# GpSimd shifts tied to vector instructions that read PSUM, with a late shift open to the vector engine, in a fused attention and MLP kernel

## The chip, the cores and the metric

The kernel runs on one NeuronCore of a Trainium2 chip. Five instruction streams run side by side and meet through semaphores: TensorE (PE, with its weight loads shown as PEld), VectorE (DVE), ScalarE (ACT), GpSimd (POOL) and SyncE (SP, which issues the DMAs). The metric is the device time of one execution in microseconds. Three runs of the kernel before gave 782.16, 782.68 and 783.34 us; their median, 782.68 us, is the time before.

## The reference

The input x has 2048 rows of 512 values. It is normalised (no learned scale), and the result xn feeds two branches that are added to x:

```
xn = layernorm(x)
q = xn @ wq            # 32 heads of 16
k = xn @ wk            # one head of 16, shared by all query heads
v = xn @ wv
p = softmax(q k^T / 4)
o = (p v) @ wo
h = gelu(xn @ w1 + b1) # 1792 wide
y = h @ w2 + b2
out = x + o + y
```

The attention is the larger part: 32 heads x 2048 queries x 2048 keys of scores, each of which needs an exponential.

## The kernel before

**Tiles.** Scores are computed transposed, 128 keys by 512 queries of one head at a time: one *tile*, one PSUM bank. There are 4 blocks of 512 queries, 8 groups of 4 heads and 16 key blocks for each, hence 2048 tiles. Three tiles make a *unit*; there are 683 units. `scores(u)` issues a unit's three matmuls (line 934) into banks 0 to 2 or 3 to 5, alternately, so a unit's banks must be emptied before the unit after next can be computed. Bank 6 collects the product with V for one group of four heads, bank 7 serves everything else (query projections, MLP).

**Two ways to the exponential.** A character of the string `DTAB` says for each unit which of its tiles take which way. Most tiles go through ScalarE's exponential (line 957, tile `E`). The others, called D tiles, go through VectorE and cost ScalarE nothing. VectorE first evicts the scores from PSUM to 16-bit integers (line 988, called p1 in the planner), which read as bf16 are a coarse exponential. Copies of this integer tile with added constants (+26, +51, +77, -26), each multiplied by V with a weight of its own and summed in PSUM, sharpen it. So a D tile feeds five matmuls (line 1001, `Dt`) against one for an `E` tile.

**The copies and the shift.** Line 1034 makes the copies on VectorE, for a *batch* of 1 to 6 D tiles at once: one instruction copies buffer 0 to buffer 1 with +26, the next copies buffers 0 and 1 to buffers 2 and 3 with +51. Then buffer 0 itself is shifted in place by -26 (line 1031), one instruction of 128x512 per tile, on GpSimd. The shift has to wait for both copies and for the matmul that reads the unshifted buffer; the fifth matmul waits for the shift. `CLOSE` letters of `DTAB` and the limit `KB` set where a batch ends.

**The planner.** `Prog.add` records each operation with its engine, dependencies, a cost (`occ`), a latency (`lat`) and an allowance; `Prog.schedule` then runs a list schedule at build time and fixes the order of instructions on each engine, and `emit` writes the streams with the semaphore waits. At run time every stream is in order: a TensorE matmul that waits for a shift holds up every matmul behind it, the next scores included. Evictions of scores have the most negative allowance on VectorE (`P1_ALLOW`), so they go first among what is ready. TensorE takes scores (kind `S`) when they are ready and otherwise products with V or side work; it gets filler matmuls (line 1305) where the planner sees a gap.

**The shifts in the planner.** Operations marked `lock` are VectorE instructions that read and write SBUF (the copies, the square of the queries, the normalisation of an output). The planner keeps them from starting before `lockend`, which is set from the end of a running shift. A shift (kind `pl`) is placed in one of two ways. When VectorE takes an operation without `lock` of at least `PL_WIN` (0.4 us in the plan), one ready shift is started beside it, and waits for the last `lock` operation or the one before it through a semaphore, the *gate*. A shift that has been ready for `PL_MAX` (2 us in the plan) is taken by GpSimd without a gate:

```
return max(o.rdy, lockend) if o.lock else o.rdy + PL_MAX if o.kind == "pl" else o.rdy
```

**The side work.** Query projections for the next block, the MLP's first product, the GELU (done by ScalarE in two stretches, after units 182 and 512, since its table must be swapped) and the MLP's second product are placed by unit numbers in `QK`, `HP`, `GU` and `YP`.

Of the kernel before, what the change touches and what calls it, by code (L numbers as in the profile page):

```python
# [33 lines left out]
S_WAIT = 0.1  # L34
P_WAIT = 0.0
PL_OCC = 0.62
PL_LAT = 0.07
PL_GATE = 0.0
PL_WIN = 0.4
PL_MAX = 2.0  # L40
PL_START = -0.07
PL_SEM = 0.16
PL_FREE = 0.135
# [12 lines left out]
DMASK = {".": (), "0": (0,), "2": (2,), "a": (0, 1), "b": (1, 2), "x": (0, 1, 2),  # L56
         "o": (0,), "t": (2,), "A": (0, 1), "B": (1, 2), "X": (0, 1, 2)}
CLOSE = "otABX"
DTAB = "tt22.to0o2.2o.2t2t02ot.toto.o2t20o.0.t02t2..2tAt.2t2222.o2t..0022t.t0t2.00.222t.22..0t02.0to02o.0..tt2t...tt2o2ot..0to0o.0.2o2t..too2o22o2t0.00o..2.2.020t2o.2.2t02ot.t22..0200o22ottA0aA20ooo222o.0t2o002o200t..020to2.oto0tt20t..2t0t0002..t0t202oo02.t2tt20.t00.0toot.tt02.o.0too.2t02o.2o2o0.t2.o22t.00to.ooot002o0t0o20....t02o.00..Bo2.tt2.2t.222..00tt.2oo.0o..tt...2oto2220o0o..o.00.o2.oto22t2..t.t.t2t2ot0.t0.0t02o0t2.t2.2o0..22.t20o.tt.o0o0.o2.t.o000220to0..t220t.2t.0.o22..o.o00o22.o.t0.o.totbA..000202ot.0t2ooo2XbX2t.0o2t02t.t200t..2ot02.ooo02o..ttt0t0.tott.oo0.t0.0t02o0.oo0t.2ot22t2oo2t..o0t.t20.ot.0o0t2t.ot2o00t.t.00.tt02t22t.t200o2.t220tt2.o0.to2t22o2.2o.0.t2oot.tt.0tt..to..."
YF = 664  # L60
Y_ALLOW = 8.0
H_ALLOW = 5.0
# [5 lines left out]
EXP_OCC = 0.0133  # L68
EXP_LAT = 0.16
Q3 = (7, 4, 2)  # L70
QK = ((48,88.7,157.4),(45,107.7,130.4),(62,118.7,153.4))
HP = ((15,19,24,26,34,41,45,46,50,52,52,63,81,89),(70.14,86,105.29,106.71,130.86,132.29,141,142.57,157.43,161.86,164.71,167.43,169.14,177.57),(290.86,291,302,305.29,307.71,324.14,341.43,344.57,345.86,358.57,372.71,377.29,378.43,389.14),(428.86,430.14,444,444.43,457.57,458.71,461.14,461.86,466.29,472.57,473.43,479.71,481.29,491))
YP = ((196,221,243,281),(347,373,383,413),(520,528,530,589),(601,635,641,654))
GU = ((182, (0, 1)), (512, (2, 3)))
# [16 lines left out]
KV_ORD = (1, 2, 3, 4, 0)  # L91
KV_DVE = ()
DU = dict(sd=50.88, sa=19.13, ag=-17.19, ln=-33.66, xn=14.6, xa=-30.73, tr=-23.53, eva=22.21, evd=14.86, k=23.66, kt=26.82, km=39.07, v=-7.76, q=15.28, vf=17.24, v0=29.19, qt0=9.89)


class _Op:
# [4 lines left out]
class Prog:  # L101
# [114 lines left out]
    def schedule(self):  # L216
# [8 lines left out]
                op.nun += 1  # L225
        engs = [e for e, _ in self.SECTIONS]
        ready = {e: [] for e in engs}
        free = {e: 0.0 for e in engs}
        for op in ops:
            if op.nun == 0:  # L230
# [2 lines left out]
        mode = None  # L233
# [14 lines left out]
        lockend, gate, prev = 0.0, None, None  # L248
# [3 lines left out]
        nfill = 0  # L252

        def seen(o):
            return max(o.rdy, lockend) if o.lock else o.rdy + PL_MAX if o.kind == "pl" else o.rdy

        while left:
            best_e, best_t = None, None
            for e in engs:
                pro = e == "pe" and self.pro_filler and not s_seen  # L260
                if not ready[e] and not pro:
                    continue
                t = max(free[e], min([seen(o) for o in ready[e]] if not pro else [0.0]))
                if best_t is None or t < best_t:
                    best_e, best_t = e, t
            assert best_e is not None, "cycle"
            e, t = best_e, best_t
            cand = [o for o in ready[e] if seen(o) <= t + 1e-9]
            if e == "pe":
                op = self.pick_pe(t, cand, ready["pe"], mode, visit, cgbusy)  # L270
                st = max([free["pe"]] + cgbusy) if mode == "col" else max([free["pe"], pend + SWITCH] + cgbusy)
# [7 lines left out]
                if op is None and self.pro_filler and not s_seen and low:  # L279
# [9 lines left out]
                    mode = "full"  # L289
# [13 lines left out]
                if FILL_GAP and tgt and low and st > FILL_FROM and lim - st > FILL_GAP:  # L303
# [13 lines left out]
                    mode = "col"  # L317
# [3 lines left out]
                if op == "idle":  # L321
                    op = None
# [4 lines left out]
            else:  # L327
                op = min(cand, key=self.due)
                if e == "dve" and not op.lock and op.occ >= PL_WIN:
                    pc = [o for o in ready["pool"] if o.kind == "pl" and o.rdy <= t + PL_GATE]  # L330
                    if pc and free["pool"] <= t + PL_GATE:
                        po = min(pc, key=self.due)
                        ready["pool"].remove(po)
                        po.start = max(t + PL_START, po.rdy, free["pool"])
                        if gate is not None:
                            po.deps.append(gate)
                            gate.need = True
                            po.start = max(po.start, gate.end + PL_SEM)
                        po.end = po.start + po.occ
                        po.vis = po.end + po.lat  # L340
                        free["pool"] = po.end
                        lockend = po.end - PL_FREE
                        po.done = True
                        order.append(po)
                        left -= 1
                        for o, cross in po.outs:
                            o.nun -= 1
                            o.rdy = max(o.rdy, po.vis if cross else po.end)
                            if o.nun == 0:
                                ready[o.eng].append(o)  # L350
                if e == "pool" and op.kind == "pl":
                    lockend = max(lockend, t + op.occ - PL_FREE)
                if e == "dve":
                    if op.lock:
                        gate = prev if prev is not None and t <= prev.end + 0.03 else op
# [7 lines left out]
            if e == "pe":  # L363
# [3 lines left out]
                if op.kind in ("pv", "side"):  # L367
# [10 lines left out]
                    mode = "col"  # L378
                    g = op.tag[0]
                if op.kind == "pv":  # L380
                    n = accn[g] = accn[g] - 1
# [7 lines left out]
                elif op.kind != "side":  # L389
# [10 lines left out]
                    mode = m  # L400
# [109 lines left out]
def bass_parallel_sum__grouped_kv_mqa__dense_activation_gelu__prompt_kernel(  # L510
# [15 lines left out]
    S, D = xf.shape  # L526
# [3 lines left out]
    NT = S // P  # L530
    DT = D // P
    FT = F // P
    TBW = 512
    NTB = S // TBW
    HG = 4
    NGR = H // HG
# [8 lines left out]
    with ExitStack() as es:  # L545
# [3 lines left out]
        x_sb = sb([P, NT, D], bf, "x_sb")  # L549
        ub = sb([P, FT, TBW], bf, "ub")  # L550
        ubs = (ub, x_sb)
# [71 lines left out]

        def B(b):
            return ("bank", b)

        def vcost(n, mode=1):
            return n / 0.96e3 / mode + 0.065

        def dve(fn, r=(), w=(), n=TBW, mode=1, allow=1.0, lat=0.16, **kw):  # L630
            return add("dve", fn, r, w, occ=vcost(n, mode), lat=lat, allow=allow, **kw)
# [27 lines left out]
        for i in range(8):  # L659
            e = X_Q[i]  # L660
# [8 lines left out]
        def setup(fn, r=(), w=(), occ=0.16, due=0.0, lat=0.1, **kw):  # L669
# [16 lines left out]
        dve(lambda e: e.memset(wqp, 0.0), w=["wqp"], n=512, due=0.1)  # L686
        setup(lambda e: e.memset(QT[:].rearrange("p g n -> p (g n)").bitcast(f32), 0.0), occ=1.9, due=DU["qt0"],
              w=[(k, g, j) for k in ("QT", "QTm") for g in range(NGR) for j in range(HG)])
# [11 lines left out]
        setup(lambda e: e.memset(crow[0:1, :], 1.13 * GAM * GAM), w=["crow"], due=10.0)  # L700
        setup(lambda e: e.memset(V1[:, :, :, Dh:32], 0.0), w=["V1"], occ=1.35, due=DU["v0"])
        for v, c in enumerate((1.0,) + SPL_C):
# [7 lines left out]
        for gl in range(2):  # L710
# [5 lines left out]
                    n=1500, due=0.01)  # L716
# [165 lines left out]
        for va, vb_ in ((0, NVA), (NVA, NT)):  # L882
# [4 lines left out]
                n=(vb_ - va) * Dh, mode=2, due=DU["vf"] + 0.1)  # L887
# [87 lines left out]
        dptr, size, base = [0, 0], [0], [0, 0]  # L975
# [30 lines left out]
        def close_batch():  # L1006
            n = len(batch)
            have = {0: 0}

            def slot(b):  # L1010
                return base[0] if b == 0 else ND + (b - 1) * NR + base[1]

            def view(b, nb):
                s = slot(b)
                step = (slot(b + 1) - s if nb > 1 else n) * TBW
                return bass.AP(Dt[:].tensor, Dt[:].offset + s * TBW, [list(Dt[:].ap[0]), [step, nb], [1, n * TBW]])

            def sums(bufs):
                for b in bufs:
                    v = 1 + SPL_K.index(have[b])  # L1020
                    for q, (t, _) in enumerate(batch):
                        gg, kt, j = tile_of(t)
                        pv_mm(gg, j, v, kt, Dt[:, slot(b) + q, :].bitcast(bf), [(("D", base[b > 0] + q), b)])

            for o, i, nb, k in SPL_STEPS:
                def keys(b):
                    return [(("D", base[b + m > 0] + q), b + m) for m in range(nb) for q in range(n)]
                if o == i:
                    for q in range(n):
                        d = Dt[:, slot(o) + q, :]  # L1030
                        add("pool", lambda e, d=d, k=k: e.tensor_scalar(d, d, 1.0, float(k), ALU.mult, ALU.add),  # L1031
                            [], [(("D", base[o > 0] + q), o)], occ=PL_OCC, lat=PL_LAT, kind="pl")
                else:
                    dve(lambda e, d=view(o, nb), q=view(i, nb), k=k: e.tensor_scalar(d, q, float(k), None, ALU.add),  # L1034
                        r=keys(i), w=keys(o), n=nb * n * TBW, mode=4, allow=1.0, kind="post", lock=True)
                for m in range(nb):
                    have[o + m] = have[i + m] + k
                sums(range(o, o + nb))
            del batch[:]
# [180 lines left out]
        for tb in range(NTB):  # L1220
# [8 lines left out]
            if tb + 1 < NTB:  # L1229
                for k in range(3):  # L1230
                    q_at(tb + 1, k, u0 + QK[tb][k], (0, 1) if k == 1 else (), (0, 1, 2, 3))
            else:
# [5 lines left out]

        for u, c in enumerate(DTAB):
            for i in DMASK[c]:  # L1240
# [103 lines left out]
```

## Time and profile before

| what | value |
|---|---|
| median of three runs | 782.68 us |
| profiled execution, its own time | 783.66 us |
| its span, first to last instruction | 781.9 us |
| PE busy | 752.8 us, 96% of the span |
| ACT busy | 745.7 us, 95% |
| DVE busy | 743.2 us, 95% |
| POOL busy | 439.8 us, 56% |
| granted TensorE clock, mean | 0.998 |
| shifts on POOL (line 1031) | 542, 423.3 us |
| copies on DVE (line 1034) | 552, 317.1 us |

"Busy" is the union of an engine's instructions in time. Successive instructions of one engine overlap by some tens of nanoseconds in the records, so a group's busy time can be less than its count times its mean. The share "idle before" of a group is the idle time of that engine just ahead of the group's instructions, with the instruction that ended most of it. An engine can also lose time while it counts as busy: an instruction that has started and is held up is shown as a longer instruction.

### The profile page before, as it was taken

What the parts mean: (1) busy time and instruction counts of PE and PEld (TensorE: products, weight loads), DVE (VectorE), ACT (ScalarE), POOL (GpSimd) and SP (SyncE); (2) the same over time, 40 slices, a digit from 0 to 9 for tenths busy, and PEclk for the clock granted to TensorE, in tenths of its full rate; (3) what the DMA queues carried; (4) which work ended last, traced back from release to release, by engine and by line L of the source; (5) the groups of instructions that cost most, each with busy time, mean ns of one, the idle gap of its engine ahead of it and who ended that gap; (6) DMA issues with size and microseconds to landing.
All of it is one profiled execution on the core that took longest, in us unless ns stands there. A gap on an engine that the chain in (4) does not pass through costs nothing.

```text
span 781.9 us, 21836 instructions
## 1 busy us (share of the span) xinstructions
PE 752.8 (96%) x9018; PEld 230.9 (30%) x9018; DVE 743.2 (95%) x1324; ACT 745.7 (95%) x747; POOL 439.8 (56%) x597
## 2 busy tenths in 40 slices
PE   7999999999989999999999999999998999999998
PEld 5332322222232222232232232322232223222223
DVE  7899999999989999999999998998998999999996
ACT  8999999999989999999999999999997999999995
POOL 5566654446474757655544456454357565756553
PEclk9999999999999999999999999999999999999999
DMA  9100101000000010100101010100100101000011
GB/s 315 47 14 9 30 10 28 12 20 17 14 23 24 7 37 16 31 23 20 32 16 29 16 37 9 33 20 10 28 3 17 36 21 37 22 24 23 23 23 36
DMA packets 32077, 23.34 MB, mean 30 GB/s; under 512 B 16369, under 2 KB 27498, under 8 KB 31978
## 3 DMA queue, kind: packets, MB, share of 16 engines
q1 hardware_dynamic: 30922, 21.90, 10.4%
q8 instruction: 72, 1.18, 0.6%
q14 instruction: 27, 0.22, 0.1%
q10 hardware_dynamic: 1056, 0.03, 0.1%
HBM read 13.08 MB, written 2.35 MB: 20 GB/s over the span
## 4 chain that ended last, share of the span: by engine, by line
PE 47%; DVE 37%; POOL 9%; ACT 5%; issue 2%; DMA 0%; SPq 0%; POOLq 0%
PE pAll L1001 23%; DVE Dt L988 17%; PE pAll L934 15%; DVE Dt L1034 14%; POOL Dt L1031 9%; PE pAll L648 8%; ACT E L957 4%; DVE Of L1046 1%; DVE ub L1137 1%; DVE x_sb L1137 1%; PE pAll L1305 1%; PE pAll L642 1%; DVE oTp L1073 1%; DVE qp L1109 1%; DMA x_sb<-in_A_x_dram 0%
## 5 line engine op out<-in xcount | busy, mean ns | idle before, releaser
L957 ACT ACTIVATE E<-pAll 128x1024 bf16<-128x1024 f32 (+1 forms) x681 | 694.9, 1173 | 22.2 <-PE pAll L934 20.3
L1031 POOL TENSOR_SCALAR Dt<-Dt 128x512 int16<-128x512 int16 x542 | 423.3, 781 | 319.7 <-DVE Dt L1034 141.7
L1001 PE MATMUL pAll<-Dt,V 128*32 128x512 bf16 x2710 | 440.0, 385 | 13.6 <-POOL Dt L1031 9.8
L988 DVE TENSOR_SCALAR Dt<-pAll 128x512 int16<-128x512 f32 (+2 forms) x530 | 358.4, 693 | 18.7 <-PE pAll L934 15.4
L1034 DVE TENSOR_SCALAR Dt<-Dt 128x1024 int16<-128x1024 int16 (+7 forms) x552 | 317.1, 602 | 1.6
L1001 PE MATMUL pAll<-E,V 128*32 128x512 bf16 x1506 | 279.0, 385 | 0.4 <-DVE Of L1046 0.2
L934 PE MATMUL pAll<-QT,KT 32*128 32x512 bf16 x2048 | 267.8, 385 | 6.4 <-DVE Dt L988 2.9
L1001 PEld LDWEIGHTS pAll<-Dt,V 128*32 128x32 bf16 x2710 | 113.1, 94 | 160.1 <-issue 71.6
L934 PEld LDWEIGHTS pAll<-QT,KT 32*128 32x128 bf16 x2048 | 67.3, 91 | 272.6 <-ACT E L957 226.0
L648 PE MATMUL pAll<-xnT,w_sb 128*32 128x512 bf16 x896 | 116.6, 383 | 0.2 <-DVE ub L1137 0.2
L1001 PEld LDWEIGHTS pAll<-E,V 128*32 128x32 bf16 x1506 | 64.7, 94 | 46.4 <-issue 35.6
L648 PE MATMUL pAll<-w_sb,ub 128*32 128x512 bf16 x448 | 72.8, 383 | 0.0
L648 PE MATMUL pAll<-w_sb,x_sb 128*32 128x512 bf16 x448 | 68.1, 383 | 0.0
L648 PE MATMUL pAll<-wop,oTp 128*32 128x512 bf16 x256 | 55.1, 383 | 0.0
L648 PEld LDWEIGHTS pAll<-xnT,w_sb 128*32 128x32 bf16 x896 | 30.3, 95 | 20.6 <-issue 10.6
L648 PE MATMUL pAll<-xnT,wq_sb 128*32 128x512 bf16 x256 | 23.3, 383 | 0.0
L1046 DVE COPY Of<-pAll 128x512 f32<-128x512 f32 x31 | 21.1, 681 | 1.1 <-PE pAll L1001 1.1
L1137 DVE TENSOR_SCALAR ub<-pAll,b1T 128x512 bf16<-128x512 f32 x28 | 20.7, 740 | 1.1 <-PE pAll L648 1.1
L1137 DVE TENSOR_SCALAR x_sb<-pAll,b1T 128x512 bf16<-128x512 f32 x28 | 20.6, 736 | 1.1 <-PE pAll L648 0.9
L648 PE MATMUL pAll<-b2row,ones 128*32 128x512 bf16 x64 | 20.1, 383 | 0.0
L648 PEld LDWEIGHTS pAll<-w_sb,ub 128*32 128x32 bf16 x448 | 18.2, 94 | 5.3 <-issue 3.6
L648 PEld LDWEIGHTS pAll<-w_sb,x_sb 128*32 128x32 bf16 x448 | 17.0, 95 | 7.5 <-issue 5.2
(120 smaller groups left out, 248.3 us busy)
## 6 DMA issues: line engine op xcount, KB each, us to landing
OfP<-Of SPq DMA_DIRECT2D x124, 32.0 KB, 2.0
rbP<-rden_rows SPq DMA_DIRECT2D x124, 32.0 KB, 1.8
w_sb<-in_B_w_dram SPq DMA_DIRECT2D x2, 1792.0 KB, 12.7
x_sb<-in_A_x_dram SPq DMA_DIRECT2D x8, 256.0 KB, 4.6
x_sb<-in_A_x_dram SPq DMA_DIRECT2D x16, 128.0 KB, 2.2
QT<-qp SPq DMA_DIRECT2D x124, 16.0 KB, 1.8
out_dram<-x_sb SPq DMA_DIRECT2D x12, 128.0 KB, 2.0
wq_sb<-in_A_wq_dram SPq DMA_DIRECT2D x1, 512.0 KB, 6.4
```

Of the source, the lines that this page charges most:

```text
L642: return add("pe", lambda e: e.matmul(o, l, rh, start=start, stop=stop, **kw), r, w, occ=occ, lat=0.23, allow=allow, **ak)
L648: add("pe", lambda e, c=c, j=j: e.matmul(o[c, :], l[:, c], rh, start=start, stop=stop, tile_position=(0, 32 * j)), r, [(k, j) for k in w] ...
L934: ins = e.matmul(o, l, rh, start=True, stop=True, tile_position=(q0, 0))
L957: o = act(lambda e: e.activation(E[:, s0:s0 + na, :], bank(b0, na).rearrange("p (a n) -> p a n", a=na), ACT.Exp, scale=LN2 / 128.0), w=[B( ...
L988: op = dve(lambda e: e.tensor_scalar(Dt[:, s:s + n, :], bank(bk, n).rearrange("p (a n) -> p a n", a=n), float(127 * 128) + SPL_D, SPL_MIN, ...
L1001: add("pe", lambda e, a, b: e.matmul(pO[32 * j:32 * j + 32, :], V1[:, v, kt, :], rhs, start=a, stop=b, tile_position=(0, 32 * j)), r=r + [ ...
L1031: add("pool", lambda e, d=d, k=k: e.tensor_scalar(d, d, 1.0, float(k), ALU.mult, ALU.add), [], [(("D", base[o > 0] + q), o)], occ=PL_OCC, ...
L1034: dve(lambda e, d=view(o, nb), q=view(i, nb), k=k: e.tensor_scalar(d, q, float(k), None, ALU.add), r=keys(i), w=keys(o), n=nb * n * TBW, m ...
L1046: dve(lambda e: e.tensor_copy(Of[:, i, :], pO), w=["O", ("Of", i)], allow=0.0)
L1073: onorm[gg - h] = onorm[gg] = dve(lambda e: e.tensor_tensor(oTp[0:n, sl, :], OfP[0:n, s, :], rbP[0:n, s, :], ALU.mult), r=keys, w=[("oTp", ...
L1109: dve(lambda e: e.tensor_copy(qp[:, s, :], pM), w=M4 + [("qp", s)], allow=EV_ALLOW)
L1137: dve(lambda e: e.tensor_scalar(ubs[tb % 2][:, ft, :], pM, b1T[:, ft:ft + 1], None, ALU.add), r=["b1T"], w=M4 + [ukey(tb, ft)], n=TBW + 57 ...
```

## The change

Four constants, the selection of shifts in the planner, the tile string and one position are changed:

- A shift is now marked `lock`, with an allowance of `PL_DUE` (3.0). GpSimd no longer takes a shift by itself: `able` gives GpSimd everything but shifts, and offers the shifts to VectorE.
- Beside a VectorE operation without `lock`, shifts are started one after another as long as at least `PL_WIN` of the operation is left. One may start up to `PL_GATE` (0.1) after the operation's start.
- A shift that has been ready for `PL_TAKE` (1.0) may be taken by VectorE, in the order of due times; it then is the same 128x512 instruction in place, issued on VectorE, and counts as `lock` like a copy.
- The latency assumed between a shift and the matmul that reads it goes from 0.07 to 0.2.
- `DTAB` is another string, and one position in `QK` goes from 153.4 to 159.4 units after the third block's start.

```diff
-PL_LAT = 0.07
-PL_GATE = 0.0
+PL_LAT = 0.2
+PL_GATE = 0.1
 PL_WIN = 0.4
-PL_MAX = 2.0
+PL_TAKE = 1.0
+PL_DUE = 3.0
...
-QK = ((48,88.7,157.4),(45,107.7,130.4),(62,118.7,153.4))
+QK = ((48,88.7,157.4),(45,107.7,130.4),(62,118.7,159.4))
...
         def seen(o):
-            return max(o.rdy, lockend) if o.lock else o.rdy + PL_MAX if o.kind == "pl" else o.rdy
+            return max(o.rdy + (PL_TAKE if o.kind == "pl" else 0.0), lockend) if o.lock else o.rdy
...
+                if e in ("pool", "dve"):
+                    able[e] = [o for o in ready["pool"] if (o.kind == "pl") == (e == "dve")] + (ready[e] if e == "dve" else [])
...
                 if e == "dve" and not op.lock and op.occ >= PL_WIN:
-                    pc = [o for o in ready["pool"] if o.kind == "pl" and o.rdy <= t + PL_GATE]
-                    if pc and free["pool"] <= t + PL_GATE:
+                    tt = t
+                    while t + op.occ - tt >= PL_WIN:
+                        pc = [o for o in ready["pool"] if o.kind == "pl" and o.rdy <= tt + PL_GATE]
+                        if not pc or free["pool"] > tt + PL_GATE:
+                            break
                         po = min(pc, key=self.due)
                         ready["pool"].remove(po)
-                        po.start = max(t + PL_START, po.rdy, free["pool"])
+                        po.start = max(tt + PL_START, po.rdy, free["pool"])
...
-                        free["pool"] = po.end
+                        free["pool"] = tt = po.end
...
-                if e == "pool" and op.kind == "pl":
-                    lockend = max(lockend, t + op.occ - PL_FREE)
+                if e == "dve" and op.kind == "pl":
+                    ready["pool"].remove(op)
+                    ready["dve"].append(op)
+                    op.eng = op.stream = "dve"
+                    op.kind, op.occ, op.lat = "post", vcost(TBW, 4), 0.16
...
-                            [], [(("D", base[o > 0] + q), o)], occ=PL_OCC, lat=PL_LAT, kind="pl")
+                            [], [(("D", base[o > 0] + q), o)], occ=PL_OCC, lat=PL_LAT, allow=PL_DUE, kind="pl", lock=True)
```

The built programs differ in these counts of instructions:

| instructions | before | after |
|---|---|---|
| shifts on GpSimd | 542 | 389 |
| shifts on VectorE | 0 | 155 |
| D tiles / E tiles | 542 / 1506 | 544 / 1504 |
| batches of 1, 2, 3, 4, 5, 6 tiles | 117, 89, 45, 16, 6, 3 | 150, 72, 41, 18, 5, 5 |
| evictions of one D tile (line 988) | 520 | 522 |
| exponentials of two banks / three banks | 521 / 152 | 523 / 150 |
| filler matmuls (line 1305) | 160 | 84 |

More of the change, by code (lines that the diff above doesn't have):

```diff
@@ L58 @@
 CLOSE = "otABX"
-DTAB = "tt22.to0o2.2o.2t2t02ot.toto.o2t20o.0.t02t2..2tAt.2t2222.o2t..0022t.t0t2.00.222t.22..0t02.0to02o.0..tt2t...tt2o2ot..0to0o.0.2o2t..too2o22o2t0.00o..2.2.020t2o.2.2t02ot.t22..0200o22ottA0aA20ooo222o.0t2o002o200t..020to2.oto0tt20t..2t0t0002..t0t202oo02.t2tt20.t00.0toot.tt02.o.0too.2t02o.2o2o0.t2.o22t.00to.ooot002o0t0o20....t02o.00..Bo2.tt2.2t.222..00tt.2oo.0o..tt...2oto2220o0o..o.00.o2.oto22t2..t.t.t2t2ot0.t0.0t02o0t2.t2.2o0..22.t20o.tt.o0o0.o2.t.o000220to0..t220t.2t.0.o22..o.o00o22.o.t0.o.totbA..000202ot.0t2ooo2XbX2t.0o2t02t.t200t..2ot02.ooo02o..ttt0t0.tott.oo0.t0.0t02o0.oo0t.2ot22t2oo2t..o0t.t20.ot.0o0t2t.ot2o00t.t.00.tt02t22t.t200o2.t220tt2.o0.to2t22o2.2o.0.t2oot.tt.0tt..to..."
+DTAB = "20t0220t2..o.02ttt.o.22.to0.2.ot00t2.tt20t.too..222ot2.t.t0.tt2tt0o2.tto.o.ott..oto2ot22.000t0..oot.ot00o.tooot0t.t.200o.0.2o2t..ooo2o20o.ot.o0o..02o..20t2..20tto0o.222o..2220oto02tA2bAoooo02t2o.t22ootoo202oo.22t.tto0t02.o20.o2.to00to..0tto0o22oo22.2tt2o.to0.0toot.tt02.t.2ooo.t202o.t00o0.t2.o22t.0oto00t020o2..o000o0oo.2...02ot00.oo...b...o.2.tt.ooo.0.22at.0t0o.t200.22toob...0t.to..ttto0t..2ootoot02.o0.o..oo2t0to0.ooo2..t02o2.20toot0.o.t220.A.o.0o0.ot.t2.2to0ott20o.2.2222o0.22.0o2ot2...ot.tt..20t02200o00..o.2X2XoBtooo2tt20tt..0o.o0t0t.o.2t2ooto2t.to22tt0t.t.o0o00o.o0.ottt2o200to.2o00.o220.o.2ttt2o2o0.0t02.t0o2.t.2ot.0to0t.2ot02o202o.2.o0ooot2t202o.0oo..o2oo.02tt.22o2.t.2o.o.."
 YF = 664
@@ L93, with vcost @@
 DU = dict(sd=50.88, sa=19.13, ag=-17.19, ln=-33.66, xn=14.6, xa=-30.73, tr=-23.53, eva=22.21, evd=14.86, k=23.66, kt=26.82, km=39.07, v=-7.76, q=15.28, vf=17.24, v0=29.19, qt0=9.89)
+TBW = 512
+def vcost(n, mode=1):
+    return n / 0.96e3 / mode + 0.065
 class _Op:
@@ L227, in schedule @@
         ready = {e: [] for e in engs}
+        able = dict(ready)
         free = {e: 0.0 for e in engs}
@@ L260, in schedule @@
                 pro = e == "pe" and self.pro_filler and not s_seen
-                if not ready[e] and not pro:
+                if e in ("pool", "dve"):
+                    able[e] = [o for o in ready["pool"] if (o.kind == "pl") == (e == "dve")] + (ready[e] if e == "dve" else [])
+                if not able[e] and not pro:
                     continue
-                t = max(free[e], min([seen(o) for o in ready[e]] if not pro else [0.0]))
+                t = max(free[e], min([seen(o) for o in able[e]] if not pro else [0.0]))
                 if best_t is None or t < best_t:
@@ L267, in schedule @@
             e, t = best_e, best_t
-            cand = [o for o in ready[e] if seen(o) <= t + 1e-9]
+            cand = [o for o in able[e] if seen(o) <= t + 1e-9]
             if e == "pe":
@@ L532, in bass_parallel_sum__grouped_kv_mqa__dense_activation_gelu__prompt_kernel @@
     FT = F // P
-    TBW = 512
     NTB = S // TBW
@@ L625, in B @@
             return ("bank", b)
-        def vcost(n, mode=1):
-            return n / 0.96e3 / mode + 0.065
         def dve(fn, r=(), w=(), n=TBW, mode=1, allow=1.0, lat=0.16, **kw):
```

## The prediction

> **What bounds the kernel now.** First the page's list of engines, then the three stretches of the span.
>
> ```profile
> PE 752.8 (96%) x9018; PEld 230.9 (30%) x9018; DVE 743.2 (95%) x1324; ACT 745.7 (95%) x747; POOL 439.8 (56%) x597
> 0.00:25.00 25.00, 18.72 (x179) 12.24 (x180) 19.17 (x56) 19.52 (x52) 13.02 (x49) 1.00 0.84 275
> 25.00:760.00 735.00, 715.07 (x8589) 211.47 (x8591) 708.93 (x1237) 712.60 (x683) 418.54 (x538) 1.00 0.09 21
> 760.00:782.00 22.00, 19.03 (x256) 7.14 (x248) 15.08 (x34) 13.56 (x14) 8.26 (x11) 1.00 0.13 36
> ```
>
> The columns after each stretch's length are busy PE, PEld, DVE, ACT and POOL, then the granted TensorE clock. In the long middle PE, DVE and ACT are all busy for 709 to 715 of 735 us, so no one engine is the bound and a share of busy time decides nothing. I therefore asked what lies inside DVE's busy time and what ends the idle time. Next, the groups of instructions with shapes kept apart, and single instructions from the timeline.
>
> ```profile
> L1034 DVE TENSOR_SCALAR Dt<-Dt 128x1024 int16<-128x1024 int16 x206 | 92.8, 463 | 0.5
> L1034 DVE TENSOR_SCALAR Dt<-Dt 128x2048 int16<-128x2048 int16 x105 | 79.4, 757 | 0.2
> L1034 DVE TENSOR_SCALAR Dt<-Dt 128x512 int16<-128x512 int16 x117 | 39.9, 350 | 0.3
> L1034 DVE TENSOR_SCALAR Dt<-Dt 128x1536 int16<-128x1536 int16 x45 | 27.4, 610 | 0.2
> L1031 POOL TENSOR_SCALAR Dt<-Dt 128x512 int16<-128x512 int16 x542 | 423.3, 781 | 319.7 <-DVE Dt L1034 141.7 <-PE pAll L1001 62.5 <-DVE Dt L988 59.0
> ...
> 300.20 0.55 DVE L1034 TENSOR_SCALAR Dt<-Dt 128x1536 int16<-128x1536 int16 x1
> 300.67 1.28 DVE L988 TENSOR_SCALAR Dt<-pAll 128x512 int16<-128x512 f32 x2
> 301.87 0.42 DVE L1034 TENSOR_SCALAR Dt<-Dt 128x1024 int16<-128x1024 int16 x1
> 302.20 0.68 DVE L988 TENSOR_SCALAR Dt<-pAll 128x512 int16<-128x512 f32 x1
> ...
> 311.92 0.68 DVE L1034 TENSOR_SCALAR Dt<-Dt 128x2048 int16<-128x2048 int16 x1
> 312.52 0.69 DVE L988 TENSOR_SCALAR Dt<-pAll 128x512 int16<-128x512 f32 x1
> 316.25 0.29 DVE L1034 TENSOR_SCALAR Dt<-Dt 128x512 int16<-128x512 int16 x1
> 316.42 0.62 POOL L1031 TENSOR_SCALAR Dt<-Dt 128x512 int16<-128x512 int16 x1 [4.72 <-DVE Dt L988]
> 316.45 0.69 DVE L988 TENSOR_SCALAR Dt<-pAll 128x512 int16<-128x512 f32 x1
> 317.05 0.29 DVE L1034 TENSOR_SCALAR Dt<-Dt 128x512 int16<-128x512 int16 x1
> ```
>
> Two things are to be seen. An undisturbed copy takes 0.29, 0.42, 0.55 and 0.68 us for 512, 1024, 1536 and 2048 elements, and the mean copy is longer by 60, 43, 60 and 77 ns. Times the counts that is 117 x 0.060 + 206 x 0.043 + 45 x 0.060 + 105 x 0.077 = 26.7 us, and with the same excess on the 79 larger copies 32 us. Counted over the records, the excess sits in 97 copies that overran by 0.34 us each (33 us), beside nearly all of which a shift was running. And a shift takes 0.62 us beside an eviction (316.42) but 0.78 us on average.
>
> The price that DVE really pays for an instruction is the spacing of starts: 0.20 us for a 512 copy (316.25 to 316.45), 0.33 for 1024, 0.47 for 1536, 0.60 for 2048, so 0.133 for each further 512, and 0.60 for an eviction.
>
> Last, who waits for whom, and two places in the timeline, both at the end of a GELU.
>
> ```profile
> ACT E L957 <- PE pAll L934: 20.3, 35, 3.6
> DVE Dt L988 <- PE pAll L934: 15.4, 24, 2.2
> PE pAll L1001 <- POOL Dt L1031: 9.8, 20, 1.4
> ...
> 225.87 5.73 POOL L1031 TENSOR_SCALAR Dt<-Dt 128x512 int16<-128x512 int16 x6
> 228.81 1.09 PE L1001 MATMUL pAll<-Dt,V 128*32 128x512 bf16 x5 [1.42 <-POOL Dt L1031]
> ...
> 233.01 1.94 ACT L957 ACTIVATE E<-pAll 128x1024 bf16<-128x1024 f32 x2 [2.04 <-PE pAll L934]
> ...
> 585.79 10.02 POOL L1031 TENSOR_SCALAR Dt<-Dt 128x512 int16<-128x512 int16 x11
> 595.16 0.39 PE L1001 MATMUL pAll<-Dt,V 128*32 128x512 bf16 x1 [0.54 <-POOL Dt L1031]
> 595.86 0.39 PE L1001 MATMUL pAll<-Dt,V 128*32 128x512 bf16 x1 [0.31 <-POOL Dt L1031]
> 597.85 1.02 ACT L957 ACTIVATE E<-pAll 128x1024 bf16<-128x1024 f32 x1 [3.63 <-PE pAll L934]
> ```
>
> The second number of a wait is how often, the third the longest. Eleven shifts follow each other from 585.79 in 10.02 us; matmuls wait for them, and since PE is in order the scores behind them come late: at 597.85 ACT has been idle for 3.63 us, its longest wait. PE was held over 0.1 us in this way at 22 places in the middle, 10.1 us together (nearly the 9.8 of the row). DVE's idle time in the middle is 735 - 708.93 = 26.1 us; 14.8 us of it begins within 3 us after one of these places, and so do 17.1 us of what ACT loses between exponentials. Matched with the planner's order, 21 of the 22 late shifts, and about 90 of the 97 slowed copies, belong to the 290 shifts without a gate of their own; the 252 gated ones account for about 7 copies and 2 us.
>
> **The change, part by part.** *No more self-starting shifts.* 290 such shifts go; all 389 left are gated. Of the 32 us in slowed copies I leave 389/252 x 2 = 3 us: gain 29 us of DVE's time. Bounds: 0 (every copy still held up) to 32.
>
> *155 shifts on DVE.* 155 x 0.20 = +31.0 us, all on an engine that is never free in the middle. Each waits for matmuls that read the old buffer, and behind it in the queue stand evictions that free score banks; it is offered only when ready for over 1 us in the plan, so I charge no wait. The bounds: 155 x 0 to 155 x 0.08 us (half of the 0.16 us by which shifts now overrun), 12 us.
>
> *Tile table.* By batch size the change in batches times its two copies: size 1, +33 x (0.20 + 0.33) = +17.5; 2, -17 x (0.33 + 0.60) = -15.8; 3, -4 x (0.47 + 0.87) = -5.4; 4, +2 x 1.73 = +3.5; 5, -2.1; 6, +5.1: together +2.8 us. Two more evictions, +1.2 us. DVE's added work is 31.0 + 2.8 + 1.2 = +35.0 us. On ACT two exponentials of two banks come and two of three go: less than 1 us saved, nothing. PE gets 8 more products on top of 4,216 and loses 76 fillers, which stand in gaps: nothing either way, as long as the clock holds at 1.00 as above with fewer of them. That fewer fillers were planned (160 to 84) says that the new order leaves PE fewer planned holes, but I price it at nothing.
>
> *PE's waits for shifts.* A shift beside an eviction takes its 0.62 us, a shift on DVE 0.20, and the new order has a GpSimd shift and its matmul with no scores between them 17 times, against 64. I let the 14.8 us of DVE's idle time go. What is late next is the scores themselves (PE idle for ACT's and DVE's evictions), the other 11.3 us. Bounds: 0 to 20 us.
>
> *Gates and the larger latency.* Semaphore waits on POOL's queue: POOL needs 389 x 0.62 = 241 us of 782, nobody queues behind it but other shifts. Nothing. *The moved position* delays one query projection by 6 units of about 1.15 us (782/683); it has 11 units left before its block begins. Nothing, or some tenths if its eviction lands in a crowded place.
>
> *Sum*, on DVE, the only engine whose work changes: busy 743.2 - 29 + 35.0 = 749.2; idle at both ends (25 - 19.17) + (22 - 15.08) = 12.7; idle in the middle 26.1 - 14.8 = 11.3. Span 773.2. ACT alone would allow 781.9 - 17.1 = 764.8, so DVE sets it. The profiled execution took 783.66 us, 1.8 over its span, and the median of the runs is 782.68, so a median lies 0.8 over this span: **774.0 us**, 1.1% less. Less than 0.2% (1.6 us) can't be told from no change here.
>
> **A rule against the rows.** The shift at 316.42 took 0.62 us beside an eviction and ended at 317.04, just ahead of the copy at 317.05, while the mean shift, copies included, takes 0.78. The Trainium skill, page "SBUF — State Buffer", section "Who interferes with whom", says why that can be: a vector instruction in a two-port mode and a GpSimd instruction exclude each other for a whole instruction, whichever starts first, and one outside these modes with at most one SBUF operand takes no part. This trace agrees. Against the change speaks another page of the Trainium skill, "Perfetto Trace Analysis", section "Optimizing Scalar/DVE Operations": a saturated DVE should shed work, and moving work between it and GpSimd may not help. With its 60 ns of overhead an instruction plus the streaming, 155 shifts would cost some 30 us (an estimate); the rows gave 31.0.
>
> **The rivals.** *DVE becomes the bound (slower).* Place: the middle; shifts and smaller batches put 35.0 us more into DVE's queue, ahead of evictions, which then come late for the next scores. If the 29 us come back but none of the 14.8 us of idle time does, the span is 749.2 + 12.7 + 26.1 = 788.0 and the median 788.8; if nothing comes back, the far end is 782.7 + 35.0 = 817.7. It decides once DVE's idle time in the middle stays over 782.68 - 0.8 - 749.2 - 12.7 = 20.0 us. For it: DVE is already busy for 96% of the middle. Against: most of its idle time follows waits that the change removes. (That work moved between these two engines may not help is the rule of the Trainium skill's "Perfetto Trace Analysis" named above.)
>
> *Waits change their name.* 55 of the 155 shifts on DVE have their matmul before the next scores; PE then waits for DVE instead of POOL. With half of the 14.8 us kept the median is 781.4, about no change. For it: the 55 tight pairs. Against: a shift on DVE takes 0.20 us and not 0.62, and nothing stretches it.
>
> *The change doesn't do what it says.* Gated shifts still run into copies: a shift (0.62) outlasts an eviction (0.60) as soon as it starts late. If a third of the 389 held up a copy by 0.17 us (316.42 began that much after the copy at 316.25), 22 us instead of 3 stay and the median is 793. Against: 252 gated shifts cost about 2 us in this trace.
>
> **How the numbers follow.** Forecast, 768 to 780: 0.66. Waits change their name, 780 to 785: 0.13 (faster 0.05, same 0.06, slower 0.02). DVE the bound, 785 to 791: 0.13. Gated shifts collide: 0.05. Better than forecast, more idle time going: 0.03. Faster 0.74, same 0.06, slower 0.20. The range 765 to 789 takes in both ends of the idle time; the likeliest case by itself is 768 to 780.
>
> **What would show it.** Right: 389 shifts on POOL with a mean near 0.64 us; the mean 1024 copy near 0.42; PE's wait for POOL under 3 us; the wait of ACT for scores well under 20.3 us; DVE busy near 749. Wrong: DVE's group of 512 shapes over 0.35 us on average (collisions), a new wait of PE for line 1034's shifts of several us, or evictions whose idle time before them (waiting for scores) stays at 15 us with DVE near 750: then the work added on DVE was not paid for.

## The result and the profile after

The changed kernel takes 756.67 us against 782.57 us for the kernel before; a second set of executions gave 757.04 against 782.74, a ratio of 0.9668 (95% interval 0.9654 to 0.9682). That is 3.3% faster. The forecast was 774.0 us with a range of 765 to 789: the direction was right, the gain was three times as large, and the time lies below the range. One execution of the first set, the profiled one, took 3,411.87 us with matmuls of about 1.5 us instead of 0.38; the other three took 756.64 to 756.70, the ratio rests on these, and the trace read here is that of the second set.

The list of engines from the page after, and the three stretches of its span (columns as before: length, then busy PE, PEld, DVE, ACT and POOL):

```profile
PE 737.2 (98%) x8950; PEld 233.4 (31%) x8950; DVE 738.2 (98%) x1511; ACT 738.1 (98%) x747; POOL 313.3 (41%) x444
0.00:25.00 25.00, 18.01 (x179) 11.95 (x180) 19.19 (x56) 19.52 (x52) 13.06 (x49) 0.86 0.85 275
25.00:735.00 710.00, 701.80 (x8537) 214.71 (x8539) 704.13 (x1421) 706.43 (x684) 296.82 (x392) 1.00 0.09 22
735.00:756.00 21.00, 17.37 (x240) 6.79 (x237) 14.85 (x36) 12.10 (x13) 3.46 (x4) 0.99 0.11 33
```

DVE is idle for 710 - 704.13 = 5.9 us of the middle, where it was 26.1. Now the groups of copies (line 1047 in the changed kernel) and shifts (line 1044), with shapes kept apart (count, busy us, mean ns, idle time ahead):

```profile
L1047 DVE TENSOR_SCALAR Dt<-Dt 128x1024 int16<-128x1024 int16 x222 | 88.9, 413 | 0.1
L1047 DVE TENSOR_SCALAR Dt<-Dt 128x2048 int16<-128x2048 int16 x90 | 61.4, 683 | 0.1
L1047 DVE TENSOR_SCALAR Dt<-Dt 128x512 int16<-128x512 int16 x150 | 41.0, 281 | 0.1
L1044 DVE TENSOR_SCALAR Dt<-Dt 128x512 int16<-128x512 int16 x155 | 39.4, 283 | 0.0
L1044 POOL TENSOR_SCALAR Dt<-Dt 128x512 int16<-128x512 int16 x389 | 296.8, 763 | 418.2 <-DVE Dt L1047 160.5 <-PE pAll L1014 77.2 <-DVE Dt L1001 48.7
```

Every mean on DVE is that of an undisturbed copy: 413 ns where it was 463, 683 for 757, 281 for 350. The 155 shifts on DVE (fourth line) cost 283 ns each in the records and DVE never stood idle ahead of them. The waits after that answer to those shown of before:

```profile
PEld pAll L1014 <- POOL Dt L1044: 6.2, 22, 0.6
DVE Dt L1001 <- PE pAll L947: 3.5, 8, 0.8
ACT E L970 <- PE pAll L947: 3.4, 8, 0.7
```

The row in which PE's matmuls waited 9.8 us for POOL is gone; what is left (6.2 us) is of weight loads, nearly all of it beside running matmuls: one gap over 0.1 us on PE is ended by a shift, of 0.13 us. The like row of weight loads before was

```profile
PEld pAll L1001 <- POOL Dt L1031: 42.8, 96, 1.7
```

ACT's waits for scores fell from 20.3 to 3.4 us, DVE's from 15.4 to 3.5.

For the account of DVE's time below I took the records in order. An instruction's *work* is the usual spacing from its start to the next one's for its shape (the lower quartile over these runs); what a spacing exceeds this by, where no gap follows, is *held up*; gaps are *idle*, and with them, as *ends*, goes what the instruction ahead of a gap shows beyond its usual spacing. Where much is held up, nearly all of it is copies and shifts (28.2 of the 30.3 us before), so it is called held-up copies below.

| kernel | median us | DVE work | held up | idle and ends |
|---|---|---|---|---|
| before | 782.7 | 701.3 | 30.3 | 46.0 |
| after | 757.0 | 736.2 | 3.3 | 11.5 |
| change | -25.7 | +34.9 | -27.0 | -34.5 |

Work, held up and idle add up to -26.6, which is the change of the profiled span (781.9 to 755.3) and that of the medians within a microsecond. Of the -34.5, recorded gaps in the middle make 20.2 (26.1 to 5.9), gaps at both ends of the span 1.4, and the ends of instructions ahead of gaps the other 12.9.

### The profile page after: what moved, and what is told of

It is laid out like the page before. It is cut to its first block, busy times and chain, and to the rows that moved or that the text cites. A ratio compares the mean times of both kernels' runs of the same rounds, so it can differ in the third digit from the quotient of the medians.

```text
span 3410.1 us, 21709 instructions
## 1 busy us (share of the span) xinstructions
PE 3402.4 (100%) x8948; PEld 426.5 (13%) x8950; DVE 795.2 (23%) x1511; ACT 808.8 (24%) x747; POOL 306.0 (9%) x444
## 4 chain that ended last, share of the span: by engine, by line
PE 99%; issue 1%; ACT 0%; DVE 0%; POOL 0%; POOLq 0%
PE pAll L1014 50%; PE pAll L947 27%; PE pAll L661 19%; PE pAll L655 2%; PE pAll L1318 1%; PE pAll L799 1%; PE pAll L1316 0%; PE pAll L1110 0%; ACT xnT L804 0%; DVE x_sb L1150 0%; PE pAll L887 0%; ACT ub L1311 0%; ACT oTp L833 0%; DVE kmr L889 0%; POOL ident L686 0%
## 5 line engine op out<-in xcount | busy, mean ns | idle before, releaser
L1014 PE MATMUL pAll<-Dt,V 128*32 128x512 bf16 x2720 | 1911.2, 1580 | 0.0
L1014 PE MATMUL pAll<-E,V 128*32 128x512 bf16 x1504 | 1209.8, 1522 | 0.0
L947 PE MATMUL pAll<-QT,KT 32*128 32x512 bf16 x2048 | 999.4, 1427 | 0.0
L1001 DVE TENSOR_SCALAR Dt<-pAll 128x512 int16<-128x512 f32 (+1 forms) x532 | 374.1, 703 | 2163.6 <-PE pAll L947 2152.3
L1044 POOL TENSOR_SCALAR Dt<-Dt 128x512 int16<-128x512 int16 x389 | 289.5, 744 | 2995.4 <-DVE Dt L1047 1157.5
L661 PE MATMUL pAll<-xnT,w_sb 128*32 128x512 bf16 x896 | 547.7, 1592 | 0.9 <-DVE x_sb L1150 0.9
L661 PE MATMUL pAll<-w_sb,x_sb 128*32 128x512 bf16 x448 | 321.1, 1597 | 0.0
L661 PE MATMUL pAll<-w_sb,ub 128*32 128x512 bf16 x448 | 310.8, 1591 | 0.0
L1047 DVE TENSOR_SCALAR Dt<-Dt 128x1024 int16<-128x1024 int16 (+6 forms) x582 | 289.5, 525 | 2.1 <-PE pAll L1014 1.6
L661 PE MATMUL pAll<-wop,oTp 128*32 128x512 bf16 x256 | 238.8, 1589 | 0.0
```

Of the source, the lines that this page charges most:

```text
L661: add("pe", lambda e, c=c, j=j: e.matmul(o[c, :], l[:, c], rh, start=start, stop=stop, tile_position=(0, 32 * j)), r, [(k, j) for k in w] ...
L947: ins = e.matmul(o, l, rh, start=True, stop=True, tile_position=(q0, 0))
L1001: op = dve(lambda e: e.tensor_scalar(Dt[:, s:s + n, :], bank(bk, n).rearrange("p (a n) -> p a n", a=n), float(127 * 128) + SPL_D, SPL_MIN, ...
L1014: add("pe", lambda e, a, b: e.matmul(pO[32 * j:32 * j + 32, :], V1[:, v, kt, :], rhs, start=a, stop=b, tile_position=(0, 32 * j)), r=r + [ ...
```

## The experiments

Two theories stood at the start. A: the rule for shifts carries the gain, since late and stretched shifts cost more than the forecast charged. B: the new tile table carries it. A third, C, on record with the first runs, says that the table is only good together with its rule.

**Rule and table crossed.** The first kernel is the planner of before with `DTAB` and `QK` of after, the second the planner of after with both of before, the third the changed kernel with two constants of before.

```diff
 # oldrule_newtab (in before)      newrule_oldtab (in after); QK goes with DTAB in both
-DTAB = "tt22.to0o2.2o..."        -DTAB = "20t0220t2..o.0..."
+DTAB = "20t0220t2..o.0..."       +DTAB = "tt22.to0o2.2o..."
 # newrule_oldlat (in after)
-PL_LAT = 0.2
-PL_GATE = 0.1
+PL_LAT = 0.07
+PL_GATE = 0.0
```

> The changed kernel itself, for a trace in which the matmuls have their usual length. Theory A (the late and stretched shifts were the whole cost, and the forecast only undervalued how far one delay spreads): slowed copies under 4 us, PE's wait for shifts under 3 us, DVE busy near 735 us or less, DVE idle in the middle under 10 us. Theory B (the new tile table itself needs less): DVE busy far under the 749 us of the forecast although copies still overrun. Time 756 to 757 us in both.

> The planner of before (shifts may start by themselves after 2 us) with the new tile table and position alone. Theory A (the rule carries the gain): 778 to 790 us, 30 us of slowed copies as before. Theory B (the table carries it): 757 to 765 us. Theory C (the table is only good with the rule for which it was chosen, neither carries it alone): 775 us or more here and also with the rule alone.

> The new rule and its constants with the old tile table and position; 334 shifts stay on GpSimd, 208 go to DVE. Theory A: 757 to 768 us, slowed copies under 4 us. Theory B: 778 us or more. Theory C: 772 to 785 us, with the slowed copies gone but idle time of DVE and ACT in their place.

> The changed kernel with the two constants of before, an assumed latency of 0.07 us between a shift and its matmul and no start after the eviction's start; the rule and the table are the new ones. If the tighter latency is what made PE wait for shifts (theory D), PE's wait for POOL returns to 8 us or more and the time to 768 us or more. If self-started shifts were the cause (A), the wait stays under 4 us and the time within 757 to 766 us, what is added being the order that no longer suits the table.

Measured: the repeated kernel 757.04 us, the new table under the old rule 806.59, the old table under the new rule 787.90, the old constants 776.35. A and B both fall as single causes (A's 757 to 766 us was missed by the old constants too), and C's main claim holds, 775 us or more on both sides, though the 787.90 lies 3 us over the range that it gave for that kernel. The accounts tell more: under the old rule the new table has 35.2 us of held-up copies and 61.9 us of idle time; under the new rule the old table has 4.4 and about 32; with the old constants it is 3.5 and 25.6, and PE's gaps that POOL ends come to 0.2 us, so theory D (the tighter latency makes PE wait for POOL) falls as well, although the time lies where it put it. The rule does away with the held-up copies whatever the table. About half or more of what the misfits lose under the new rule stands in one place, the start of the second GELU: ACT waits there for 15.0 us with the old table (30.9 us slower than the changed kernel), for 9.5 with the old constants (19.3 slower) and for 8.4 with two letters exchanged (10.8 slower), and not at all in the changed kernel. From the timelines of the old table, then of the exchanged letters (below), both under the new rule:

```profile
585.20 1.02 ACT L970 ACTIVATE E<-pAll 128x1024 bf16<-128x1024 f32 x1 [15.01 <-PE pAll L947]
586.24 1.28 ACT L1162 ACT_TABLE_LOAD   x1
```

```profile
571.04 1.02 ACT L970 ACTIVATE E<-pAll 128x1024 bf16<-128x1024 f32 x1 [8.42 <-PE pAll L947]
```

ACT stands still for 15.0 us ahead of its last exponential before the activation table is swapped, while DVE and PE still work off copies and the MLP's first product, which the GELU needs.

**The order kept, the gates left out.** Crossed kernels are planned anew, so every order changes. The next ones keep the order of instructions on every engine and change one thing in it. Theory E says that the order was never the trouble, only shifts that run at other moments than it foresees; F, that the order is the gain.

```diff
 # after_nogate; after_halfgate does it for every second shift
                         if gate is not None:
-                            po.deps.append(gate)
-                            gate.need = True
                             po.start = max(po.start, gate.end + PL_SEM)
```

> The changed kernel with its order of instructions on every engine kept; only the semaphore wait that ties each of the 389 GpSimd shifts to a VectorE instruction is left out, so a shift starts as soon as its data allow. Theory E (the order was never the trouble; shifts that run at other moments than the order foresees are): 772 to 790 us, slowed copies back to 20 us or more, PE's wait for POOL lines and DVE's idle time up with it. Theory F (the gain is the better order from the new table and from 155 shifts on VectorE, the gates are an extra): under 763 us.

> The changed kernel with its order kept and every second of the 389 gates left out. Without any, slowed copies grew by 28 us and the time by 28 us. If each copy held up is time lost on an engine that has no slack (theory E): slowed copies 14 to 20 us and 768 to 774 us. If the copies lost are taken up by slack until there are many: under 764 us.

Measured: 784.77 us without any gate, 765.07 with half of them. Same instructions, same order, and the whole gain is gone with the 389 semaphore waits. DVE's account shows where: held up 3.3, 11.7 and 31.6 us with all, half and none of the gates, work 736 us in each, idle 11.5, 11.0 and 10.6. The time rises by 8.0 and 27.7 us, the held-up copies by 8.4 and 28.3: microsecond for microsecond. Theory E's other half did not come: it had PE's waits for POOL and DVE's idle time going up as well, and without gates neither does. Leaving out half of the gates cost less than I had expected (14 to 20 us of slowed copies), and 765.07 lies between the two ranges, but no slack swallowed any of it. The rows without gates, and the middle stretch:

```profile
L1045 DVE TENSOR_SCALAR Dt<-Dt 128x1024 int16<-128x1024 int16 x222 | 95.5, 442 | 0.1
L1045 DVE TENSOR_SCALAR Dt<-Dt 128x512 int16<-128x512 int16 x150 | 49.2, 336 | 0.1
L1042 DVE TENSOR_SCALAR Dt<-Dt 128x512 int16<-128x512 int16 x155 | 44.3, 314 | 0.0
25.00:760.00 735.00, 714.90 (x8517) 215.47 (x8516) 729.57 (x1417) 715.80 (x683) 298.53 (x391) 1.00 0.09 21
```

DVE is busy for 729.57 of 735 us, and 28 us more of that than in the changed kernel is waiting. The same stretch of DVE's and POOL's instructions, in the timeline after and then without gates:

```profile
107.33 0.73 POOL L1044 TENSOR_SCALAR Dt<-Dt 128x512 int16<-128x512 int16 x1 [0.92 <-DVE Dt L1047]
107.50 0.68 DVE L1001 TENSOR_SCALAR Dt<-pAll 128x512 int16<-128x512 f32 x1
108.10 0.95 DVE L1047 TENSOR_SCALAR Dt<-Dt 128x512 int16<-128x512 int16 x3
108.81 0.73 POOL L1044 TENSOR_SCALAR Dt<-Dt 128x512 int16<-128x512 int16 x1 [0.74 <-DVE Dt L1047]
108.97 0.68 DVE L1001 TENSOR_SCALAR Dt<-pAll 128x512 int16<-128x512 f32 x1
```

```profile
109.96 1.53 POOL L1042 TENSOR_SCALAR Dt<-Dt 128x512 int16<-128x512 int16 x2 [0.87 <-DVE Dt L1045]
110.13 0.68 DVE L999 TENSOR_SCALAR Dt<-pAll 128x512 int16<-128x512 f32 x1
110.73 1.36 DVE L1045 TENSOR_SCALAR Dt<-Dt 128x512 int16<-128x512 int16 x3
111.85 1.52 POOL L1042 TENSOR_SCALAR Dt<-Dt 128x512 int16<-128x512 int16 x2 [0.36 <-DVE Dt L1045]
112.02 0.68 DVE L999 TENSOR_SCALAR Dt<-pAll 128x512 int16<-128x512 f32 x1
```

With gates a shift runs from 107.33 to 108.06, the eviction covers it, and the three copies behind it (one row, which names the size of the first) take 0.95 us. Without, the second shift follows the first at once, runs to 111.49 into the same three copies, and they take 1.36: the second of them, of 1024 elements, lasts until 111.77 and takes 0.83 us instead of 0.42. The Trainium skill, page "SBUF — State Buffer", section "Who interferes with whom", says of a DVE instruction in a two-port mode and a GpSimd instruction that the one that starts first keeps the other out for the whole instruction; the pair of rows agrees.

**Gates for the kernel before, and its late shifts on DVE.** The first kernel adds to each of the 290 self-started shifts a wait for the last DVE instruction that the planner had finished by then; the second issues these 290 on DVE at their place in the order.

```diff
 # before_gated
                 if e == "pool" and op.kind == "pl":
                     lockend = max(lockend, t + op.occ - PL_FREE)
+                    done = [o for o in order if o.eng == "dve" and o.end + PL_SEM <= t]
+                    if done:
+                        op.deps.append(done[-1])
+                        done[-1].need = True
 # before_dve290; late.append(op) in the same branch, and after the schedule:
+        for o in pr.late:
+            o.eng = o.stream = "dve"
```

> The kernel before with its order of instructions on every engine and its tile table kept; each of the 290 shifts that GpSimd started by itself now also waits for the last VectorE instruction that the planner had finished by then. All 542 shifts stay on GpSimd. Theory E: 757 to 772 us, slowed copies under 12 us. Theory F: 778 us or more. If the gates hold but the shifts come later than the matmuls want them, PE's wait for POOL stays near 10 us while the slowed copies go: 772 to 780 us.

> The kernel before with its order and its tile table kept, but the 290 shifts that GpSimd started by itself are issued by VectorE at their place in the order; the 252 gated ones stay. VectorE's work grows by 290 x 0.20 = 58 us to about 759 us. If the idle time of before came from late and stretched GpSimd shifts (theory E), slowed copies fall to under 4 us, PE's wait for POOL to under 1 us and VectorE's idle time with the drained ends of instructions ahead of gaps from 46 to under 22 us: 778 to 787 us. If most of that idle time belongs to the old order itself (theory G), it stays over 33 us: 793 us or more.

Measured: 785.57 us with the added gates, by its number theory F's end, right after the run without gates had spoken for E. Held-up copies fell only from 30.3 to 23.3 us, and PE waited more:

```profile
ACT E L961 <- PE pAll L938: 23.1, 39, 3.8
PE pAll L1005 <- POOL Dt L1035: 12.7, 28, 1.4
```

9.8 us became 12.7, idle time and ends went from 46.0 to 56.3. So E needs a correction: a gate by itself is not the remedy. The 290 were placed in the plan without an eviction to run beside, and held to their moment they come later to the matmuls and still run into copies. Nor was the order without fault, as the crossed tables show.

With the 290 shifts on DVE: 786.99 us. Work rose to 758.9 us (+57.6; 290 x 0.20 = 58), held-up copies fell to 4.7, and idle time and ends from 46.0 to 17.6, which is theory E's end of the expectation (the 4.7 just over its 4, the time at the very end of its range). The waits:

```profile
ACT E L959 <- PE pAll L936: 19.3, 49, 3.4
DVE Dt L990 <- PE pAll L936: 5.1, 11, 0.9
PE pAll L1003 <- POOL Dt L1033: 0.2, 1, 0.2
PEld pAll L936 <- DVE Dt L990: 84.3, 184, 1.0
```

DVE's waits for scores went from 15.4 to 5.1 us. So in the old order, with the old table, the self-started shifts cost DVE 26 us in held-up copies; doing them on DVE takes away another 28 us of idle time, and costs about as much as both. That the shifts had caused all of these 28 us is not shown, since a DVE with 58 us more to do may fill its gaps in any case: the gaps of ACT (34.1 and 34.2 us in all) and of PE (26.3 and 25.9) did not shrink in this run. ACT's wait stayed near 20 because its scores now wait for evictions: weight loads for scores wait 84.3 us for them, where it was 11.3.

**The 155 shifts given back to GpSimd.** The order kept, each shift that DVE had taken is issued by GpSimd, held until the DVE instruction ahead of its place is done; then every third of them only.

```diff
 # after_pool155, in a loop over the planned operations; after_pool51 does it for every third
 ...
+            if o.eng == "dve" and o.kind == "post" and o.allow == PL_DUE:
+                o.eng = o.stream = "pool"
+                if before is not None:       # the DVE instruction ahead
+                    o.deps.append(before)
+                    before.need = True
 ...
```

> The changed kernel with its order kept, but the 155 shifts that VectorE had taken are issued by GpSimd, each held until the VectorE instruction ahead of its old place is done. VectorE loses 31 us of work. If VectorE's work is what bounds the changed kernel and the place of a shift matters little: 735 to 750 us. If a shift beside whatever comes next holds up copies and matmuls (theory E): 775 us or more, with 15 us or more of slowed copies from these 155 alone.

> The changed kernel with its order kept, but every third of the 155 shifts on VectorE is issued by GpSimd (51 of them). With all 155 there, PE waited 29 us for POOL in stretches over 0.1 us and VectorE's idle time grew by 76 us, 2.6 us for each. If that factor holds for a third: PE's wait 8 to 11 us, idle time 20 to 30 us more, VectorE's work 10 us less, time 768 to 785 us. If delays only grow so when they crowd: under 762 us.

Measured: 816.92 us for 155, 773.50 for 51. The waits of PE and ACT, with 51 and then with 155:

```profile
ACT E L970 <- PE pAll L947: 16.2, 23, 3.6
PE pAll L1014 <- POOL Dt L1044: 12.6, 22, 1.8
```

```profile
PE pAll L1014 <- POOL Dt L1044: 30.5, 63, 2.3
ACT E L970 <- PE pAll L947: 48.4, 60, 6.5
```

DVE's work falls by 10.5 and 31.1 us, and its idle time rises by 19.0 and 75.9, for PE's gaps of 12.7 and 29.2 us that end with a shift. One microsecond in which PE waits costs DVE 1.5 at the small dose and 2.6 at the large; the factor of 2.6 that I had carried over to the small dose was too high, and PE's wait of 12.7 us was over the 8 to 11 that I gave, so the time fell into its range by two errors that offset each other.

**Two letters exchanged.** Units 340 and 341 of the table, `o.` to `.o`, planned anew.

```diff
-DTAB = "...o.2.tt.o..."   # "o." at unit 340
+DTAB = "....o2.tt.o..."
```

> The changed kernel with two neighbouring letters of the tile table exchanged (units 340 and 341), planned anew. Work on every engine changes by under 5 us. If the table was only good by its counts: 757 to 762 us. If any other table misfits the planner's order, as the crossed pairs of rule and table suggest: 765 to 785 us, all of it idle time on ACT and DVE, with slowed copies still under 4 us.

Measured: 767.80 us. Work +3.4 us, held-up copies 3.3 as after, idle and ends +7.3 us; the wait of 8.42 us shown above, at the second GELU, is most of what this kernel loses. A table that differs in two letters is worth 10.8 us less, which puts the 31 us between old and new table under the new rule into proportion: the table suits one order of instructions, at that boundary above all. The fillers that the planner places tell of it roughly, before a run: under the new rule 84, 176, 284 and 288 of them (new table, exchanged letters, old table, old constants) go with 11.5, 18.8, about 32 and 25.6 us of idle time and ends. Whether the old table could be refitted to the new rule by moving only the GELU or the MLP's products was not tried.

## Why the prediction was wrong

**The bound.** Right in kind: the middle had no one bound, DVE's busy time held 30 us of waiting, and what was late on POOL stalled PE, then ACT and DVE. After the change DVE is the bound, as forecast: held-up time adds to the time one to one.

**DVE's added work, +35.0 us.** Measured +34.9. **Held-up copies, -29 us.** Measured -27.0, and 3.3 left where 3 were left. **The 155 shifts without a wait.** Right: 0.0 us of idle time ahead of them.

**PE's waits for shifts, and 14.8 us of idle time with them.** This is the step that failed, by size. The waits went as foreseen (22 gaps, 10.1 us, to one of 0.13 us), but idle time and ends fell by 34.5 us and not by 14.8. I had counted DVE's recorded gaps within 3 us of one of the 22 places. The larger part of what that left out stood in no term: an instruction ahead of a gap shows its drained end, or its own hold-up, as busy time, 10.9 us before and none after, so DVE's busy time came out at 738.2 us and not at 749.2. Of the 17.9 us by which the span (755.3) is shorter than the forecast's 773.2, this busy time is 11.0, idle time in the middle 5.4 (5.9 where 11.3 were to stay), idle time at both ends 1.5. The bound I gave (0 to 20 us) was too narrow for the same reason.

How much of the 34.5 us the late shifts themselves had caused is shown only within limits. The run with them on DVE, in the same old order, gives 28.4 us, part of which the added work may have filled. By the 1.5 to 2.6 us of DVE's idle time for each microsecond of PE's waits, from the runs with 51 and 155 shifts given back, the 10 us that went would make 15 to 26 us, an estimate. A longer reach of each delay adds little: 17.4 of the 26.1 us of gaps in the middle begin within 10 us of one of the 22 places.

**The table, +2.8 us, and fewer planned fillers, nothing.** Also mis-sized. The counts were right, but a table is more than its counts: the old one under the new rule gives 787.9 us, so the forecast's likeliest case would have been wrong with it. The rest of the idle time that vanished, 34.5 - 28.4 = 6.1 us or more, I put down to the new order by difference; it isn't shown alone. The fillers (160 to 84, against 284 for the old table under the new rule) pointed that way and I priced them at nothing.

**ACT alone would allow 764.8 us.** Wrong by the same count: ACT's gaps shrank by 19.0 us (34.1 to 15.1 in all), near the 17.1, but its busy time fell as well, by 7.6 (745.7 to 738.1), with the ends ahead of its gaps, and so the time passed under that floor.

**The rivals.** DVE as the bound: came true without the loss, since the idle time in the middle fell to 5.9 us and not to the 20.0 at which it decides. The rule of the Trainium skill's page "Perfetto Trace Analysis", that moving work between DVE and GpSimd may not help, agrees with the kernel before (290 shifts on DVE: 787.0 us), and not with the changed one, where 155 shifts on DVE are worth 59.9 us in the order that was made for them. Waits change their name: no, PE's gaps of over 0.1 us that wait for DVE's shifts are absent. Gated shifts collide: no, 3.3 us.

**Signs.** The mean 1024 copy near 0.42 us: 0.413. Shifts on POOL with a mean near 0.64 us: no, 0.763, since 243 of the 389 start inside a copy, 0.16 us after its start, and wait there (0.841 us on average, the others 0.633); no gap of PE that a shift ends is over 0.13 us, and what is held up on DVE stays at 3.3 us. DVE busy near 749: 738.2, the ends ahead of gaps again. The moved position and the larger latency alone were not separated beyond the run with the old constants.

## What to carry to other kernels

When two engines exclude each other, look for the loss inside the victim's busy time: compare each shape's mean with its undisturbed time, and look at what the instructions ahead of gaps show beyond their usual spacing, which is idle time under another name. What in-order queues make of it downstream takes a run that keeps the order and moves only the suspects. Tie the weaker engine's instruction by a semaphore to a partner that leaves it room; starting it later, at a moment without such a partner, is not enough, and starting it as soon as its data allow costs as much as the whole plan gains. Here a table that suits one planner was worse than the old pair under the other, both ways, so judge rule and table together, and test them apart.

## What was unexpected

The same instructions in the same order, with 389 semaphore waits fewer, are 27.7 us slower: without the waits nothing is left of the gain. And an exchange of two letters of 683 moved the time by 10.8 us, with 3.4 us more work on DVE and no more copies held up than before the exchange.
